# Two adds of batch 0 moved from VectorE to GpSimd, and new places for steps in a hand-written order (hourglass attention, then ELU layer, one Trainium2 core)

## Chip, cores and metric

The kernel runs on one NeuronCore of a Trainium2 chip. Its time is the device time of one launch in microseconds (us), median of several runs. Five engines work side by side, each through its own queue in order: TensorE (in the profile PE, its weight loads PEld), VectorE (DVE), ScalarE (ACT), GpSimd (POOL) and SyncE (SP, which here only issues transfers). They wait for each other by semaphores.

## What is computed

Inputs are q, k, v of 8 batches, 8 heads, 576 positions, 64 values, all float32, and two weight matrices of 512x2048 and 2048x512.

```python
q_d = q.reshape(B, H, Sd, 4, D).mean(axis=3)      # k_d, v_d likewise: 144 coarse positions
out_d = softmax_attention(q_d, k_d, v_d)          # scale 1/8
out_up = np.repeat(out_d, 4, axis=2)              # coarse part, each row four times
mask = np.abs(pos[:, None] - pos[None, :]) < 4
out_local = softmax_attention(q, k, v, mask)      # local part: a band of 7 keys
x = (out_up + out_local) as [4608, 512]           # heads side by side
h = x @ w_in
g = np.where(h > 0, h, np.exp(np.minimum(h, 0)) - 1)
out = g @ w_out
```

The sum `out_up + out_local` is the "add of the coarse to the local part" that the change speaks of.

## The kernel before

A unit of the attention is one pair of heads of one batch, `(b, j)` with b from 0 to 7 and j from 0 to 3. For each pair the kernel

- loads q and k (`load_qk`, or `load_cast`, a transfer issued by GpSimd that converts to float16 on its way) and v (`load_v`, then `cast_v` on GpSimd, line 242);
- transposes q and k on TensorE (`transposes`, lines 263 to 285) and copies the result out of PSUM on ScalarE or VectorE (lines 298, 305);
- makes scores (lines 348 to 392), exponentials on ScalarE (372, 402), and in batches 1 to 7 a multiplication with the band mask on VectorE (422);
- sums denominators on TensorE and takes reciprocals on VectorE (478 to 491 in batch 0, 437 to 452 later) and spreads them over all rows (496, 508, copies 798 and 516);
- multiplies with v (551, 558 in batch 0; 531, 539 later), normalises on VectorE (568, 584) into a float16 tile `ln`, and adds the coarse to the local columns into `xt` (574 in batch 0, 604 later).

The dense layer takes blocks of 512 tokens. `mm1(t, fc)` multiplies `xt(t)` with 128 columns of w_in (line 619 for block 0, 640 for others), then ScalarE takes an exponential `e` (644) and VectorE makes the ELU in two steps (645, 646) into `gt`. `mm2(t, i)` multiplies a quarter of `gt` with w_out (660). For block 0 the first two accumulators are filled ahead (`ahead`, line 815, four calls for the four pairs of heads).

Batch 0 runs through a front of its own in halves of 288 positions: `first_transposes`, `first_scores`, `first_v`, `first_dens`, `first_spread`, `first_outputs`, `first_normalise`. The last four have an index i; i of 0 and 1 are the pairs (0,1) and (2,3) of the first half, i of 2 and 3 the same pairs of the second half. `normalise_half` makes the adds of batch 0, and line 573 takes VectorE or GpSimd for each by a list of eight entries: entries 0 to 3 are the four i of batch 0, entries 4 to 7 are the four pairs of batch 1 (line 603, for the columns that fall into block 1).

`keep(t, n)` puts work on TensorE that nothing reads: n matmuls of 512 zero columns (line 679), or for a float16 tile 4n small transposes (line 682). The numbers n are in `FK`.

PSUM holds few tiles. The tag `two` gives two large buffers in turn once `close_front` has run, for transposed q and k, scores, spread reciprocals, `lg` (outputs) and `vs`. The tags `hp` and `misc` have two banks each.

The order of all work is written out by hand. Each step is given a time by `at(time, step)`, the steps are sorted by it, and each engine's queue follows from that order. The times themselves are nothing that the chip sees. `F` and `FK` hold those of batch 0, `PLAN` those of batches 1 to 3 (tr transposes, sc scores, cast, dn denominators, vs sums of v, sp spread, out outputs), `MM1` and `MM2` those of the dense layer, and the loads of w_out (`load_wo`) have a list of their own.

Of the kernel before, what the change touches and what calls it, by code (L numbers as in the profile page):

```python
# [15 lines left out]
B, H, S, D = 8, 8, 576, 64  # L16
# [53 lines left out]
def kernel(  # L70
# [9 lines left out]
    nc = tc.nc  # L80
# [343 lines left out]
    def by_pe(b):  # L424

        return b in [0, 1, 2]
# [137 lines left out]
    def normalise_half(js, g, lg):  # L564
        z, n = js[-1] + 1, HB + SH
        ln = sb.tile([128, RW], FP16, tag="ln", bufs=2, name="ln")
        ln = h2(ln[:])
        nc.vector.tensor_tensor(
            out=ln, in0=g2(lg[:], 0, n), in1=RB[0][:, js[0] : z, n * g : n * g + n], op=AB.mult
        )  # L570
        parts = ((0, 0, HB, 0),) if g == 0 else ((0, 0, TBLK - HB, HB), (1, TBLK - HB, HB, 0))
        for t, a, b_, to in parts:
            eng = nc.vector if t == 0 and [1, 1, 1, 0, 0, 0, 0, 1][2 * g + js[0] // 2] else nc.gpsimd
            eng.tensor_tensor(
                out=xt(t)[:, js[0] : z, to : to + b_ - a].rearrange("p j (u f) -> p j u f", f=4),
                in0=ln[:, :, a:b_].rearrange("p j (u f) -> p j u f", f=4),
                in1=_rep4(ln[:, :, HB + a // 4 : HB + b_ // 4]), op=AB.add,
            )

    def normalise(b, j, lg):  # L580
        rcb = RB[b]
        ln = sb.tile([128, RW], FP16, tag="ln", bufs=2, name="ln")
        if by_pe(b):
            nc.vector.tensor_tensor(  # L584
                out=h2(ln[:]), in0=g2(lg[:], 0, HB + SH), in1=h2(rcb[:, j, :]), op=AB.mult
            )
        else:
            nc.vector.tensor_tensor(
                out=ln[:, S:RW], in0=lg[:, HB : HB + SD], in1=rcb[:, j, S:RW], op=AB.mult
            )  # L590
            nc.vector.tensor_tensor(  # L591
                out=h2(ln[:, 0:S]), in0=g2(lg[:], 0, HB), in1=h2(rcb[:, j, 0:S]), op=AB.mult
            )
        t0 = S * b
        while t0 < S * (b + 1):
            t = t0 // TBLK
            t1 = min(TBLK * (t + 1), S * (b + 1))
            a, z = t0 - S * b, t1 - S * b
            if by_pe(b) and a < HB < z:
                z, t1 = HB, S * b + HB  # L600
            h = a // HB if by_pe(b) else 0
            la, ga = (a + SH * h, HB + HB * h + a // 4) if by_pe(b) else (a, S + a // 4)
            eng = nc.vector if (b, t) == (1, 1) and [1, 1, 1, 0, 0, 0, 0, 1][4 + j] else nc.gpsimd
            eng.tensor_tensor(  # L604
                out=xt(t)[:, j, t0 - TBLK * t : t1 - TBLK * t], in0=ln[:, la : la + z - a],
                in1=_rep4(ln[:, ga : ga + (z - a) // 4]), op=AB.add,
            )
            t0 = t1
        st.pop((b, j))
# [63 lines left out]
    Z = sb.tile([128, 512], FP16, tag="Z", bufs=1, name="Z")  # L673
# [165 lines left out]

    at(-100, first)  # L840
    at(-65, second)
    F = dict(T=[-41.13, -39.95, -36.66, -32.16], S=[-39.2, -35.63, -33.39, -30.84], Z=[-32.52, -32.14, -32.14, -28.4], V=[-33.32, -30.92, -30.71, -27.94], P=[-29.75, -28.02, -20.88, -18.53], O=[-30, -26.95, -20.73, -13.92], N=[-28.12, -24.72, -19.09, -13.8], H=[-24.18, -20.45, -18.09, -17.91], lv=[-52.45, -36.44, -34.49, -32.17], cv=[-36.2, -33.27, -32.43, -29.76], lw=[-30, -29.11, -20.29, -11.97], rp=[-28.54, -23.88, -22.41, -14.05], D=[-32.62, -29.37, -29.34, -24.56], wi=[-33.19, -32.56, -30.01, -29.05], cf=[-29.29], k=[-41.47, -35.38, -33.37, -28.21])
    FK = dict(Tq=[1, 0, 0, 0], Tk=[0, 0, 2, 0], S=[1, 0, 2, 1], Z=[1, 0, 2, 0], P=[0, 1, 0, 0], O=[1, 4, 0, 2], D=[0, 0, 0, 0])
    for j in range(NPAIR):
        at(F["T"][j], first_transposes, j, (FK["Tq"][j], FK["Tk"][j]))
        at(F["S"][j], first_scores, j, 0, FK["S"][j])
# [24 lines left out]
        spread_copy(b, j, rb, copy)  # L871

    MM1 = [[-14.19, 1.09, 0.706], [19.14, 0.992], [35.73, 1.018], [51.52, 1.02]]
    MM2 = [[14.98, 0.794], [34.5, 1.095], [51.68, 1.02]]

    def mm1_at(t, i):
        if t == 0:
# [10 lines left out]
    def load(n):  # L888
# [2 lines left out]
            load_v(*pairs[n])  # L891

    PLAN = {
        1: dict(tr=[-12.21, -5.594, -1.76, -1.482], sc=[-7.07, 0.103, 0.888, 2.276], cast=[-23.96, -13.31, -12.32, 1.701], dn=[16.38], vs=[15.62], sp=[18.61, 18.14, 18.46, 18.98], out=[18.98, 18.52, 18.54, 18.99], so=[10.57], si=[10.03]),
        2: dict(tr=[8.521, 19.14, 20.81, 24.84], sc=[16.66, 21.68, 23.15, 26.21], cast=[6.002, 15.82, 19.12, 20.36], dn=[28.71], vs=[29.1], sp=[30.02, 30.15, 29.43, 32.38], out=[30.72, 32.86, 33, 33.03], so=[17.79], si=[28.4]),
        3: dict(tr=[25.32, 29.24, 30.74, 34.58], sc=[28.69, 32, 36.48, 37.89], cast=[21.15, 25.5, 25.89, 28.85], dn=[40.9], vs=[40.84], so=[41.77], si=[43.95], out=[46.72, 47.24, 48.76, 48.78]),
    }
    LATER = dict(tr=[-27.78, -24.81, -17.34, -16.19], sc=[-25.74, -22.03, -14.56, -12.79], cast=[-32.93, -27.69, -22.54, -19.07], dn=[-10.25], vs=[-10.47], so=[-9.791], si=[-6.96], out=[-4.288, -4.511, -3.148, -3.906])
    LAST = dict(tr=[-27.36, -24.54, -17.71, -14.25], sc=[-25.67, -22.06, -15.67, -11.26], cast=[-32.18, -27.83, -24.84, -20.85], dn=[-9.492], vs=[-9.098], so=[-9.367], si=[-5.664], out=[-2.829, -4.665, -4.912, -2.635])
# [3 lines left out]
    for b in range(1, B):  # L903
        p = PLAN[b]
        for j in range(NPAIR):
            n = NPAIR * (b - 2) + j
# [18 lines left out]
                at(p["out"][js[0]], pair_outputs, b, js)  # L925
    for n, x in enumerate([-8.454, -6.202, 3.581]):
        at(x, load, n)
    for n, x in enumerate([-21.48, -3.996, 1.576, 2.844]):
        at(x, load_wo, n)
    for t in range(NT):  # L930
        for i in range(16):
# [35 lines left out]
```

## Time and profile before

| | |
|---|---|
| median of 3 runs | 357.72 us (356.89 to 359.48) |
| the profiled execution | 356.68 us, span from first to last instruction 354.8 us |
| mean granted TensorE clock | 0.995 |
| DVE, ACT, POOL busy | 247.1, 200.0, 167.6 us |
| TensorE idle in the first 140 us / after it | 12.9 / 3.3 us |

The last row is the length of the stretches less PE's busy time in them. The profile is of one execution. It tells per instruction when it began, how long it took, how long its engine sat idle before it and what ended the wait. The chain of waits follows the work back from the last instruction; "issue" in it is time for which no releaser is seen. Some loads of this part, from the queue of transfers that GpSimd issues: w_in is loaded in four parts (WI, issued between 15.42 and 19.95 us), w_out in four (WO, issued at 35.86, 47.38, 51.78 and 53.50).

### The profile page before, as it was taken

Reading aid. Unit: us, or ns where it says so; the run is one execution under the profiler, and the core shown is the slowest. Engines: PE = TensorE matmul, PEld = TensorE weight load, DVE = VectorE, ACT = ScalarE, POOL = GpSimd, SP = SyncE. Lnnn points to the kernel's source line nnn. Section 1 sums busy time; section 2 is a strip of 40 time slices with the busy share of each in tenths; the row PEclk is TensorE's granted clock in tenths of the full one; section 3 lists DMA queues with packets and bytes.
Section 4 is the critical chain, followed back from the end, with each engine's and each line's share of the span. In section 5 each row is a group of like instructions: output and inputs, shape, how many; then the busy total and the mean of one; then the engine's idle time right before and its main releaser. Section 6 shows DMA issues by size and latency. Waiting matters only on the chain.

```text
span 354.8 us, 8863 instructions
## 1 busy us (share of the span) xinstructions
PE 338.6 (95%) x3520; PEld 191.6 (54%) x3520; DVE 247.1 (70%) x452; ACT 200.0 (56%) x368; POOL 167.6 (47%) x305
## 2 busy tenths in 40 slices
PE   8887998899979999999999999999999999999996
PEld 4665886555555555555555555555555544444443
DVE  2316998676898868887997799879766855555510
ACT  3572798457775754677476736773664444444421
POOL 4534658596877744954595459846200500000000
PEclk9998999999999999999999999999999999999999
DMA  8999999999794958686968698461004010010012
GB/s 180 179 191 200 189 201 217 226 216 229 170 203 92 228 147 164 144 219 152 188 166 217 151 179 202 110 142 35 31 32 117 32 59 30 31 59 30 31 59 89
DMA packets 100322, 49.12 MB, mean 138 GB/s; under 512 B 81770, under 2 KB 95290, under 8 KB 100282
## 3 DMA queue, kind: packets, MB, share of 16 engines
q1 hardware_dynamic: 94442, 42.20, 53.1%
q0 software_dynamic: 5600, 6.26, 10.6%
q8 instruction: 27, 0.44, 0.6%
q10 hardware_dynamic: 240, 0.11, 0.2%
q14 instruction: 13, 0.11, 0.1%
HBM read 42.24 MB, written 9.62 MB: 146 GB/s over the span
## 4 chain that ended last, share of the span: by engine, by line
PE 88%; DVE 5%; ACT 4%; issue 2%; DVEq 0%; ACTq 0%
PE op L660 35%; PE hp L640 31%; PE sc L382 3%; PE lg L531 2%; PE hp L619 2%; PE sc L679 2%; PE tqk L268 2%; ACT pex L402 1%; PE sc L392 1%; PE vs L338 1%; DVE ln L584 1%; DVE gt L646 1%; PE lg L539 1%; PE den L437 1%; ACT e L644 1%
## 5 line engine op out<-in xcount | busy, mean ns | idle before, releaser
L660 PE MATMUL op<-WO,gt 128*128 128x512 f16 (+2 forms) x592 | 145.3, 374 | 0.0
L644 ACT ACTIVATE e<-hp 128x512 f16<-128x512 f32 x144 | 86.3, 602 | 91.8 <-PE hp L640 78.2
L640 PE MATMUL hp<-xt,WI 128*128 128x512 f16 x512 | 132.0, 380 | 0.7 <-DVE xt L604 0.6
L646 DVE SCALAR_TENSOR_TENSOR gt<-hp,e 128x512 f16<-128x512 f32 x144 | 99.6, 692 | 6.4
L660 PEld LDWEIGHTS <-gt 128*128 128x128 f16 x592 | 55.2, 98 | 61.6 <-issue 0.9
L645 DVE TENSOR_SCALAR e<-e 128x512 f16<-128x512 f16 x144 | 60.1, 417 | 40.2 <-ACT e L644 39.5
L640 PEld LDWEIGHTS <-WI 128*128 128x128 f16 x512 | 55.0, 114 | 48.2
L604 POOL TENSOR_TENSOR xt<-ln 128x128 f16<-128x128 f16 (+10 forms) x62 | 37.4, 632 | 48.7 <-DVE ln L591 41.1
L402 ACT ACTIVATE pex<-sc 112x576 f16<-112x576 f32 x112 | 50.0, 528 | 10.6 <-PE sc L392 10.5
L329 POOL TENSOR_TENSOR t<-qt 128x288 f32<-128x288 f16 x27 | 18.2, 672 | 39.4 <-ACT qt L298 39.4
L422 DVE TENSOR_TENSOR pex<-pex,MASK 112x1152 f16<-112x1152 f16 x28 | 23.8, 851 | 15.5 <-ACT pex L402 15.3
L242 POOL CAST v<-v 112x768 f16<-112x768 f32 x32 | 27.0, 844 | 12.2 <-DMA v<-in_v_dram 12.2
L666 ACT COPY os<-op 128x512 f32<-128x512 f32 (+2 forms) x37 | 21.4, 578 | 18.3 <-PE op L660 18.1
L323 DVE TENSOR_REDUCE kd<-kt 128x144 f16<-128x576 f16 x28 | 20.8, 744 | 1.1 <-ACT kt L305 1.1
L298 ACT COPY qt<-tqk 128x576 f16<-128x576 f16 x28 | 18.0, 644 | 5.9 <-PE tqk L268 5.1
L205 POOL CAST k<-k 96x768 f16<-96x768 f32 x24 | 20.4, 848 | 0.1
L205 POOL CAST q<-q 96x768 f16<-96x768 f32 x24 | 19.7, 821 | 0.2 <-issue 0.2
L382 PEld LDWEIGHTS <-kt 64*112 64x112 f16 x336 | 11.3, 127 | 12.4 <-issue 11.6
L619 PE MATMUL hp<-xt,WI 128*128 128x256 f16 x128 | 17.0, 283 | 0.5 <-DVE v L217 0.4
L382 PE MATMUL sc<-qt,kt 64*112 64x96 f16 x336 | 14.7, 217 | 1.5 <-ACT pex L402 1.3
L331 POOL TENSOR_TENSOR qd<-t 128x144 f16<-128x144 f32 x27 | 14.0, 519 | 2.1
L591 DVE TENSOR_TENSOR ln<-lg,rcb 128x576 f16<-128x576 f32 x20 | 15.0, 748 | 0.0
(111 smaller groups left out, 291.5 us busy)
## 6 DMA issues: line engine op xcount, KB each, us to landing
v<-in_v_dram SPq DMA_DIRECT2D x30, 336.0 KB, 6.0
out_dram<-os SPq DMA_DIRECT2D x35, 256.0 KB, 2.1
q<-in_q_dram SPq DMA_DIRECT2D x25, 288.0 KB, 3.5
k<-in_k_dram SPq DMA_DIRECT2D x25, 288.0 KB, 4.3
rcb<-rd SPq DMA_DIRECT2D x10, 360.0 KB, 5.2
WI<-in_moe_w_in_dram POOLq DMA_DIRECT2D x4, 512.0 KB, 9.6
WO<-in_moe_w_out_dram POOLq DMA_DIRECT2D x4, 512.0 KB, 7.8
q<-in_q_dram POOLq DMA_DIRECT2D x7, 144.0 KB, 7.1
```

The lines of the kernel that those rows point to most:

```text
L205: nc.gpsimd.tensor_copy(out=x[:], in_=src)
L242: nc.gpsimd.tensor_copy(out=v16[:], in_=v32[:].rearrange("p (e c) d -> p c e d", e=2))
L382: nc.tensor.matmul(sc[e][0:KW, a : a + QB], s["kt"][r, KO - PAD + QB * c :][:, 0:KW], s["qt"][c][r], start=True, stop=True,)
L402: nc.scalar.activation(out=s["p"][0:rows, e, :, a : a + n], in_=g2(sc[0:rows], a, n), func=AF.Exp, scale=SCALE / 16 if b and a == HB else ...
L422: nc.vector.tensor_tensor(out=to, in0=to, in1=mk2, op=AB.mult)
L604: eng.tensor_tensor(out=xt(t)[:, j, t0 - TBLK * t : t1 - TBLK * t], in0=ln[:, la : la + z - a], in1=_rep4(ln[:, ga : ga + (z - a) // 4]), ...
L619: nc.tensor.matmul(FS[i][:, 256 * f : 256 * f + 256], w_in(dc, 2 * n + f), xts[0][:, dc, 256 * h : 256 * h + 256], start=(f == dc == 0), s ...
L640: nc.tensor.matmul(hp, w_in(dc, fc), xts[t][:, dc, :], start=(dc == 0), stop=(dc == DMC - 1),)
L644: nc.scalar.activation(out=e, in_=hp, func=AF.Exp)
L645: nc.vector.tensor_scalar(out=e, in0=e, scalar1=1.0, scalar2=-1.0, op0=AB.min, op1=AB.add)
L646: nc.vector.scalar_tensor_tensor(out=to, in0=hp, scalar=0.0, op0=AB.max, in1=e, op1=AB.add)
L660: nc.tensor.matmul(op_[:, a:z], gts[t][:, fc, 128 * tt : 128 * tt + 128], WO[:, fc, a:z], start=(fc == 0), stop=(fc == FCN - 1),)
```

## The change

Two entries of the list on lines 573 and 603 go from 1 to 0, the tables of times get new values, and three numbers of `FK` change.

```diff
--- before.py
+++ after.py
@@ -570,7 +570,7 @@
         )
         parts = ((0, 0, HB, 0),) if g == 0 else ((0, 0, TBLK - HB, HB), (1, TBLK - HB, HB, 0))
         for t, a, b_, to in parts:
-            eng = nc.vector if t == 0 and [1, 1, 1, 0, 0, 0, 0, 1][2 * g + js[0] // 2] else nc.gpsimd
+            eng = nc.vector if t == 0 and [0, 1, 0, 0, 0, 0, 0, 1][2 * g + js[0] // 2] else nc.gpsimd
             eng.tensor_tensor(
                 out=xt(t)[:, js[0] : z, to : to + b_ - a].rearrange("p j (u f) -> p j u f", f=4),
                 in0=ln[:, :, a:b_].rearrange("p j (u f) -> p j u f", f=4),
@@ -600,7 +600,7 @@
                 z, t1 = HB, S * b + HB
             h = a // HB if by_pe(b) else 0
             la, ga = (a + SH * h, HB + HB * h + a // 4) if by_pe(b) else (a, S + a // 4)
-            eng = nc.vector if (b, t) == (1, 1) and [1, 1, 1, 0, 0, 0, 0, 1][4 + j] else nc.gpsimd
+            eng = nc.vector if (b, t) == (1, 1) and [0, 1, 0, 0, 0, 0, 0, 1][4 + j] else nc.gpsimd
             eng.tensor_tensor(
                 out=xt(t)[:, j, t0 - TBLK * t : t1 - TBLK * t], in0=ln[:, la : la + z - a],
                 in1=_rep4(ln[:, ga : ga + (z - a) // 4]), op=AB.add,
@@ -839,8 +839,8 @@
 
     at(-100, first)
     at(-65, second)
-    F = dict(T=[-41.13, -39.95, -36.66, -32.16], S=[-39.2, -35.63, -33.39, -30.84], Z=[-32.52, -32.14, -32.14, -28.4], V=[-33.32, -30.92, -30.71, -27.94], P=[-29.75, -28.02, -20.88, -18.53], O=[-30, -26.95, -20.73, -13.92], N=[-28.12, -24.72, -19.09, -13.8], H=[-24.18, -20.45, -18.09, -17.91], lv=[-52.45, -36.44, -34.49, -32.17], cv=[-36.2, -33.27, -32.43, -29.76], lw=[-30, -29.11, -20.29, -11.97], rp=[-28.54, -23.88, -22.41, -14.05], D=[-32.62, -29.37, -29.34, -24.56], wi=[-33.19, -32.56, -30.01, -29.05], cf=[-29.29], k=[-41.47, -35.38, -33.37, -28.21])
-    FK = dict(Tq=[1, 0, 0, 0], Tk=[0, 0, 2, 0], S=[1, 0, 2, 1], Z=[1, 0, 2, 0], P=[0, 1, 0, 0], O=[1, 4, 0, 2], D=[0, 0, 0, 0])
+    F = dict(T=[-40.88, -39.39, -36.09, -31.59], S=[-38.63, -35.07, -32.82, -29.94], Z=[-31.95, -31.57, -31.56, -27.84], V=[-32.75, -30.35, -30.14, -27.19], P=[-29.2, -27.45, -20.31, -17.62], O=[-29.43, -26.38, -20.16, -13.36], N=[-27.33, -24.16, -19.23, -13.23], H=[-23.61, -19.88, -17.52, -17.2], lv=[-52.73, -36.61, -34.54, -32.22], cv=[-35.63, -32.7, -31.61, -29.19], lw=[-29.43, -28.54, -19.72, -11.4], rp=[-27.17, -23.16, -21.13, -13.34], D=[-32.05, -28.8, -28.77, -24], wi=[-32.62, -31.99, -29.44, -28.48], cf=[-28.72], k=[-35.99, -34.56, -32.8, -27.19])
+    FK = dict(Tq=[1, 0, 0, 0], Tk=[0, 0, 3, 0], S=[1, 0, 2, 1], Z=[1, 0, 2, 0], P=[0, 1, 0, 0], O=[1, 3, 0, 0], D=[0, 0, 0, 0])
     for j in range(NPAIR):
         at(F["T"][j], first_transposes, j, (FK["Tq"][j], FK["Tk"][j]))
         at(F["S"][j], first_scores, j, 0, FK["S"][j])
@@ -871,7 +871,7 @@
         spread_copy(b, j, rb, copy)
 
     MM1 = [[-14.19, 1.09, 0.706], [19.14, 0.992], [35.73, 1.018], [51.52, 1.02]]
-    MM2 = [[14.98, 0.794], [34.5, 1.095], [51.68, 1.02]]
+    MM2 = [[14.98, 0.794], [34.5, 1.091], [51.68, 1.02]]
 
     def mm1_at(t, i):
         if t == 0:
@@ -891,9 +891,9 @@
             load_v(*pairs[n])
 
     PLAN = {
-        1: dict(tr=[-12.21, -5.594, -1.76, -1.482], sc=[-7.07, 0.103, 0.888, 2.276], cast=[-23.96, -13.31, -12.32, 1.701], dn=[16.38], vs=[15.62], sp=[18.61, 18.14, 18.46, 18.98], out=[18.98, 18.52, 18.54, 18.99], so=[10.57], si=[10.03]),
-        2: dict(tr=[8.521, 19.14, 20.81, 24.84], sc=[16.66, 21.68, 23.15, 26.21], cast=[6.002, 15.82, 19.12, 20.36], dn=[28.71], vs=[29.1], sp=[30.02, 30.15, 29.43, 32.38], out=[30.72, 32.86, 33, 33.03], so=[17.79], si=[28.4]),
-        3: dict(tr=[25.32, 29.24, 30.74, 34.58], sc=[28.69, 32, 36.48, 37.89], cast=[21.15, 25.5, 25.89, 28.85], dn=[40.9], vs=[40.84], so=[41.77], si=[43.95], out=[46.72, 47.24, 48.76, 48.78]),
+        1: dict(tr=[-12.26, -5.594, -4.144, -1.294], sc=[-7.07, 0.103, 0.888, 5.814], cast=[-24.58, -13.94, -12.95, 1.024], dn=[16.38], vs=[16.2], sp=[18.91, 18.14, 18.46, 18.98], out=[18.98, 18.52, 18.54, 18.99], so=[11.7], si=[10.03]),
+        2: dict(tr=[8.521, 19.14, 20.81, 24.93], sc=[16.66, 21.68, 23.3, 26.36], cast=[6.002, 15.72, 19.12, 20.36], dn=[28.71], vs=[29.1], sp=[30.02, 30.15, 29.43, 32.38], out=[30.72, 32.86, 32.86, 33.03], so=[18.95], si=[33.02]),
+        3: dict(tr=[25.32, 29.24, 30.74, 34.58], sc=[28.69, 32, 36.48, 37.89], cast=[21.15, 25.5, 25.89, 28.85], dn=[40.9], vs=[40.84], so=[41.03], si=[43.42], out=[46.54, 47.06, 48.57, 48.6]),
     }
     LATER = dict(tr=[-27.78, -24.81, -17.34, -16.19], sc=[-25.74, -22.03, -14.56, -12.79], cast=[-32.93, -27.69, -22.54, -19.07], dn=[-10.25], vs=[-10.47], so=[-9.791], si=[-6.96], out=[-4.288, -4.511, -3.148, -3.906])
     LAST = dict(tr=[-27.36, -24.54, -17.71, -14.25], sc=[-25.67, -22.06, -15.67, -11.26], cast=[-32.18, -27.83, -24.84, -20.85], dn=[-9.492], vs=[-9.098], so=[-9.367], si=[-5.664], out=[-2.829, -4.665, -4.912, -2.635])
@@ -925,7 +925,7 @@
                 at(p["out"][js[0]], pair_outputs, b, js)
     for n, x in enumerate([-8.454, -6.202, 3.581]):
         at(x, load, n)
-    for n, x in enumerate([-21.48, -3.996, 1.576, 2.844]):
+    for n, x in enumerate([-21.48, -4.346, 1.576, 2.844]):
         at(x, load_wo, n)
     for t in range(NT):
         for i in range(16):
```

What becomes of the order, step by step:

- Adds: entries 0 and 2 go to GpSimd, so the adds of i=0 (128x576 elements) and i=2 (128x448) of batch 0. The entries of batch 1 keep their values.
- Filling work: `first_transposes(2)` gets 12 small transposes for 8; `first_outputs(1)` three matmuls of 512 columns for four; `first_outputs(3)` none for two.
- Front, SP's queue: the constant VR (7 KB) is loaded behind v of pair 1 and not ahead of it.
- Front, PE's and ACT's queues: `first_v(2)` goes ahead of `first_scores(3, 0)`. VectorE: the small reduction for the constant FOUR (line 752) goes behind the first `ln`.
- Front, GpSimd's queue: the add of i=0, then the constant FOUR, now stand ahead of `load_cast(1, 0)`. `load_wo(0)` goes ahead of `load_cast(1, 2)`; the adds of i=2 and `cast_v(1, 1)` go ahead of `load_cast(1, 3)`.
- Batch 1: `pair_transposes(1, 2)` goes ahead of `mm1(0, 9)` and `mm1(0, 10)`. `pair_scores(1, 3)` goes behind `mm1(0, 15)`. `v_batch(1)` goes behind `mm2(0, 1)`. `cast_v(1, 3)` goes ahead of `load_wo(2)`.
- Batch 3: `pair_outputs(3, (2, 3))` goes ahead of `mm2(1, 13)`.
- The other new times (those of `first_transposes` among them) leave the order of each engine's instructions as it was.

## Prediction

> **What bounds the kernel now.** I read the page's busy times and slices first, then the chain of waits, then windows of the front, then each engine's queue in order of time.
>
> ```profile
> PE 338.6 (95%) x3520; PEld 191.6 (54%) x3520; DVE 247.1 (70%) x452; ACT 200.0 (56%) x368; POOL 167.6 (47%) x305
> PEclk9998999999999999999999999999999999999999
> q8 instruction: 27, 0.44, 0.6%
> PE 88%; DVE 5%; ACT 4%; issue 2%; DVEq 0%; ACTq 0%
> ```
>
> TensorE sets the time: 95% busy, 88% of the chain. Its idle time is 12.9 us before 140 us and 3.3 us after, so a change of order can win or lose only in the first 140 us. Every edit that moves an engine's instructions but one lies before 63 us; the exception is mm2(1, 13) at 138.5. One slice has a lower clock. The third line is PE's own instructions: 27 packets, 0.44 MB, so 16 KB each, for 3520 loads and 3520 matmuls, some 260 a packet.
>
> The chain in the front (start, length, what):
>
> ```profile
> 23.34 0.14 PE rb L496
> 23.48 1.14 issue
> 24.61 0.45 PE rb L496 x9
> ...
> 29.10 0.03 PE den L485 x2
> 29.13 1.96 issue
> 31.09 0.30 PE den L485 x6
> ```
>
> Two stops of 1.14 and 1.96 us in the middle of a row of matmuls, with no releaser. They are waits for instructions. In the trace's list of weight loads, 221, 349 and 477 loads stand ahead of the places where PE resumes at 17.47, 24.62 and 31.09: 128 matmuls with their loads, one packet, apart. The packets of the instruction queue land at 16.10, 23.04 and 29.54, each 1.4 to 1.6 us ahead of the resuming. The windows around the second stop (us, PE, PEld, DVE, ACT, POOL busy, clock, DMA):
>
> ```profile
> 27.71:31.12 3.41, 1.45 (x46) 0.81 (x45) 2.20 (x3) 0.48 (x2) 0.00 (x0) 1.00 1.23 196
> 31.12:34.53 3.41, 3.41 (x44) 2.68 (x44) 1.20 (x3) 0.76 (x1) 2.16 (x4) 0.50 1.25 222
> 34.53:37.94 3.41, 3.27 (x70) 2.77 (x68) 3.21 (x6) 1.60 (x3) 3.33 (x7) 1.00 1.19 162
> ```
>
> After a stretch with PE busy for 1.45 of 3.41 us, the clock is halved for 3.41 us: 1.7 us lost. Behind that VectorE binds until 41.5, PE again until 48.3, then ScalarE's exponentials alternate with PE until 57.7.
>
> ```profile
> 36.38 0.29 DVE L645 TENSOR_SCALAR e<-e 128x512 f16<-128x512 f16 x1
> 39.13 0.74 DVE L323 TENSOR_REDUCE qd<-qt 128x144 f16<-128x576 f16 x1
> ...
> 54.83 1.25 ACT pex L402 x3
> 56.12 0.46 PE sc L382 x11
> 56.71 1.00 PE hp L619 x8
> 57.74 0.67 PE tqk L268 x12
> ```
>
> **The change part by part**, against the profiled execution (356.68: span 354.8 plus 1.9 around it).
>
> *Fills in the front.* Eight small transposes (L682) take 0.55 on the chain, so four more cost 0.27. They stand between packet borders 93 and 221: PE reaches border 221 no sooner than its packet, and all the loss until then is eaten by the wait at 24.62, whose end depends on the packet alone (it starts 4.7 after the crossing at 17.47, in the company of the w_in loads, which are the same in both kernels). The same border then comes four matmuls earlier in the work, so four L558 of 0.02 each follow the wait. At the second stop it comes three earlier (one fill is gone): three L485 at half clock, 0.05 each, are left over. Sum +0.1. If packets came at once the cost were 0.27; if the border fell badly, 0.3. The dropped fill of i=1 (0.26) ends in the same stop: nothing. The two of i=3 (0.59) are followed by a wait of matmul hp at 37.53 for gt L646 (until 37.47), and qt L298 before it feeds only qd L323, which VectorE reaches at 39.13: nothing.
>
> *Two adds.* VectorE loses 0.76 (L574, 128x576, at 27.49) and 0.63 (128x448, at 34.88). The first lies ahead of an idle 0.72 us. The second lies ahead of rcb L798 (35.42), which would end 0.35 earlier; but e at 36.38 follows ScalarE's e (35.75 to 36.36), which follows PE. So no gain, unless PE's part shrinks, then up to 0.6. On GpSimd, rows of L574 are 0.95 for 448 columns and 0.39 to 0.42 for 128, so 576 take 1.2 as an estimate: from 27.4 to 28.6 with GpSimd idle, read by PE's hp at 31.39, 2.8 spare. The second runs from some 36.0 (behind three transfers' issue) with its 128-column partner until 37.5, and `cast_v(1, 1)` and the adds of i=3 follow; mm1(0, 8) reads them at 44.92, the adds end by 41.5.
>
> What it costs is VectorE's time beside it. Step e (L645) is 0.28 to 0.30 in all 65 cases with no GpSimd instruction beside it, and with an add of L604 beside it 0.29 to 0.86, mean 0.59 over 15. Beside the add of L574 in this front the two rows are 0.28 and 0.29, by luck of the moment.
>
> ```profile
> 137.56 2.64 POOL L604 TENSOR_TENSOR xt<-ln 128x320 f16<-128x320 f16 x4 [4.47 <-DVE ln L591]
> 138.28 0.76 DVE L645 TENSOR_SCALAR e<-e 128x512 f16<-128x512 f16 x1
> ```
>
> In the changed order GpSimd works without rest from 36 to 42, where three e stand at 36.38, 38.21 and 40.45, all on VectorE's binding stretch. Bounds: none meets, 0; all three at the worst row, 1.7. I take two at the mean excess of 0.30: +0.6. The Trainium skill, "GPSIMD Engine Reference", section 8, says that GpSimd shares its SBUF interfaces with VectorE and contends with VectorE's two-port modes and two SBUF inputs; it speaks against the change. The trace agrees for e (by the rule the term lies in the upper half, by the two rows of L574 at 0); gt (L646) is 0.69 in all its rows beside GpSimd or not, so gt costs nothing here.
>
> *Loads moved.* VR goes behind v(0,1) on SP's queue and takes over its wait for an earlier transfer; IND and the next v stand behind that wait. VR is read at 16.14, and IND, queued behind it, landed at 14.9: nothing. `load_cast(1, 0)` was issued at 19.95 and 20.59, but its packets (768 bytes) began only at 29.9, behind WI; now it waits for the add and FOUR, and is issued at 29.4 to 30.7. Behind the waiting add on GpSimd's queue are FOUR, this load and `cast_v(1, 0)`, which waited until 31.97 for its data anyway. The load is read by tqk L263 at 36.71 (36.2 now). Casts issued between 30 and 40 took 4.6 to land: 35.3, hidden. The casts of pairs 2 and 3 go behind WO's part 0 (128 packets, some 3 us) and two adds; the first landed near 38.6, lands near 42 and is read at 45.8, the last is read at 49.2, issued at 39: hidden. FOUR is read at 64. WO of part 2 goes 1.0 later, behind a cast (0.84) and its 0.18; it landed at 59.4 and is read at 61.6; part 3 landed at 62.0 and is read at 63.14. Some 0.6 later it still lands in time: nothing, else up to 1.
>
> *Batch 1.* `pair_transposes(1, 2)` comes 1.8 earlier; ScalarE then reaches e of (0, 11) when PE ends it (49.28, before 49.40), so kt L305 and sc at 51.19 come 0.1 earlier: −0.1. (In the front, `first_v(2)` puts a copy of 0.36 ahead of an exponential whose first reader stands behind the stop at 24.62: nothing.) `pair_scores(1, 3)` and `mm1(0, 15)` change places. Before, PE waits 0.64 and more for the exponentials of pair 2 (until 56.07), then hp (56.71) covers the wait for pair 3's. Now hp goes into the first gap, sc still starts at 56.1, but ScalarE makes e of (0, 15), 0.61, ahead of pair 3's exponentials, and tqk needs their buffer: 57.1 plus 0.9, so 58.0 for 57.74. +0.3. The swap of vs and mm2(0, 1) and the one at 138.5 (lg's buffer was free at 138.36) cost nothing.
>
> Sum: +0.1 +0.6 −0.1 +0.3 = +0.9, so 357.6 for this execution. It lies 1.04 below the median, so 358.6.
>
> The Trainium skill, "TensorE: Matmul & The Clock Gate", section "What's actually happening", says that the window of activity is 3.413 us and runs freely. The half-clock row agrees in length (3.41); the sentence before that an idle window is needed does not, since PE worked 1.45 us in it. By a free phase the 1.7 us come and go between executions of one kernel.
>
> **The rivals.**
>
> *Slower: the first load of batch 1 comes late.* Place: tqk L263, k's part at 36.9 us, with mm1(0, 2) and all of PE behind it. For it: the casts' median over the whole span is 7.2 from issue, and the old load took 12.5 from 20.59 to 33. Against: what delayed the old one was WI, gone by 30.2. It decides if it lands after 36.9, and makes the kernel slower by over 1% past 39.6, 8.9 behind its issue at 30.7. Price: at 7.2 (37.8), 0.9; at 12.5 (43.1), 6.2: 359.5 to 364.8. Chance of over 1%: 0.11.
>
> *Faster: the second stop vanishes.* Its packet waits 4.0 us from crossing to start, in the company of w_in. If GpSimd's later load frees the engines before 28.66, the stop (1.96) and the half clock (1.7) go: 3.7 off the median, 354.0, and the other terms add −0.4 to +0.9: 353.6 to 354.9. Against: the old load's packets began at 29.9, after the instruction packet. 0.08, half of it beyond one per cent.
>
> *No change: VectorE's relief is worth its contention.* If the meetings of e miss (0) and the 0.35 of rcb count, +0.3 −0.35: 357.7. It is nearest to the two rows of L574. 0.11.
>
> *The change does less than it says.* For batch 1 it does: its four entries keep their values, so no add of batch 1 moves. That is in the sum.
>
> **How the numbers follow.** Forecast 0.70, no change 0.11, late load 0.11, vanished stop 0.08. Predicted 358.6. Low end: sum at −0.4 (no meetings, rcb counted, no loss at sc) on the lowest run shown, 356.89: 356.5. High end: port 1.7, WO 1.0, sc 0.3 and front 0.3 give +3.3 on the median: 361.0. The 0.19 of the two outer rivals lie outside. Within one per cent (3.6 us, about what a measurement of this kernel can tell from no change) lie forecast, no change and half the vanished stop, 0.70 + 0.11 + 0.04: faster 0.04, same 0.85, slower 0.11.
>
> **What would show it.** Right: stops at the same two borders, resuming near 24.6 and 31.1; e between 36 and 41 longer than 0.30 at least twice; tqk of (2, 0) some 0.3 behind its old place relative to sc of (1, 3) ending. Wrong: PE waiting at tqk near 36 for a transfer; a stop of another length, or another half-clock stretch; e at 0.29 throughout and VectorE still earlier at 41.5.

## The result, and the profile after

The changed kernel takes 360.37 us (median of 20 runs, 358.20 to 361.60), the kernel before, run beside it, 358.35 (20 runs). The ratio is 1.0066, 95% interval [1.0046, 1.0086]: slower by two thirds of a per cent, about 2.4 us. (Ratios here leave out runs more than 1.5% above the fastest of their kernel; where that takes out half of a changed kernel's runs, the median over all stands beside it.) The profiled execution took 360.88 us, its span 359.0.

First the page of the changed kernel: busy times, granted clock by slices, the instruction queue, the chain's shares.

```profile
PE 338.8 (94%) x3521; PEld 192.3 (54%) x3521; DVE 246.5 (69%) x450; ACT 199.8 (56%) x368; POOL 170.2 (47%) x307
...
PEclk9998799999989999999999999999999999999999
...
q8 instruction: 27, 0.44, 0.5%
...
PE 80%; DMA 6%; DVE 6%; ACT 2%; issue 2%; POOL 1%; SPq 0%; DVEq 0%; POOLq 0%; ACTq 0%
```

PE is busy for as long as before (338.8 against 338.6), and the span is 4.2 longer. Its idle time in the first 140 us is 16.9 us for 12.9: nearly the whole difference of the two executions is idle PE there. In the chain, transfers have come in (6%) and PE's share has gone from 88% to 80%. Of the 4.2 us, only 2.0 are the difference of the medians: the profile of before is of an execution 1.67 us faster than its median of 358.35, that of the changed kernel of one 0.51 slower than its own.

Next the chain through the front (start, length, what), and PE's rows in order of time around the same place:

```profile
18.80 11.89 DMA WI<-in_moe_w_in_dram
30.70 3.80 issue
34.50 1.01 PE hp L619 x4
```
```profile
27.59 0.21 PE L478 MATMUL den<-pex,IND 112*32 112x72 f16 x1 [0.93 <-issue]
27.60 0.27 PE L485 MATMUL den<-pex,IND 96*32 96x72 f16 x8
27.80 0.63 PE L619 MATMUL hp<-xt,WI 128*128 128x256 f16 x4
...
34.50 1.01 PE L619 MATMUL hp<-xt,WI 128*128 128x256 f16 x4 [5.23 <-issue]
```

The same second group of L619 before, then the last issue of w_in and the times from issue to landing of its four parts, first before, then after:

```profile
33.75 0.97 PE L619 MATMUL hp<-xt,WI 128*128 128x256 f16 x4
...
19.21 0.74 POOL L137 DMA_DIRECT2D WI<-in_moe_w_in_dram  x1
DMA to landing us min/median/max: 5.5/9.6/12.4
...
20.30 0.75 POOL L137 DMA_DIRECT2D WI<-in_moe_w_in_dram  x1
DMA to landing us min/median/max: 7.7/11.2/14.1
```

"Border n" is the place in PE's work with n weight loads ahead of it; PE crosses it when it starts the next one. The two stops before were at borders 349 and 477. As in the forecast, the start of the packet for border 349 is counted from PE's crossing of border 221, one packet earlier.

The two stops for instructions are gone but for 0.93 us at border 477: the packets land at 13.93, 18.36 and 26.07 (16.10, 23.04 and 29.54 before), the first two ahead of PE. The first `ahead` starts at 27.80, 3.5 us earlier than before. The second starts at 34.50, later than before (33.75): PE stands still for 5.23 us. The view names no releaser, but the semaphores kept in the trace do: here PE's queue waits for those of the second, third and fourth part of w_in, and the last one landed at 34.4, issued at 20.30. This group reads columns of the first part alone, as the first `ahead` does, and the first `ahead` waited for the first part alone. The same wait stands in the kernel before; there PE came to it, delayed by its stops, when w_in had landed (31.6; the forecast had it gone by 30.2). So the stops and the wait for w_in lay over each other, and w_in was late, too: the cast of v(0, 0), which stands ahead of w_in on GpSimd's queue, began at 13.67 and not at 11.55, since its data landed later.

The windows around it (us, busy PE, PEld, DVE, ACT, POOL, granted clock, DMA), and one later pair:

```profile
29.48:32.89 3.41, 0.00 (x0) 0.00 (x0) 0.91 (x1) 0.07 (x1) 3.08 (x6) 1.00 1.24 206
32.89:36.30 3.41, 1.80 (x16) 1.48 (x17) 0.15 (x1) 0.00 (x0) 1.35 (x3) 0.50 1.35 211
36.30:39.71 3.41, 3.41 (x53) 2.58 (x51) 2.30 (x4) 1.11 (x3) 1.94 (x4) 0.50 1.11 201
39.71:43.12 3.41, 3.41 (x32) 3.36 (x32) 3.27 (x7) 2.85 (x5) 1.69 (x3) 1.00 0.99 149
101.10:104.50 3.40, 2.40 (x22) 1.59 (x22) 3.37 (x6) 1.76 (x4) 3.13 (x8) 1.00 1.22 236
104.55:107.96 3.41, 3.41 (x38) 1.95 (x39) 2.48 (x4) 1.28 (x3) 1.58 (x5) 0.51 1.53 212
```

One wait of 5 us in one piece leaves PE idle for a whole window and for half of the next, and the clock is halved for two windows (6.8 us, the first 1.6 of them still within the wait) instead of one. At 104.6 a third half-clock window follows a stretch with PE busy for 2.40 of 3.40 us. It is not the change's own: eight of the fourteen profiles of this study have 3.4 or 6.8 us of half clock near 100 us, among them z2, z3 and y4 below, which are variants of the kernel before; the profile of before has none.

Last, VectorE's e of block 0 and GpSimd's instructions beside it, in order of time:

```profile
47.80 1.40 POOL L329 TENSOR_TENSOR t<-qt 128x288 f32<-128x288 f16 x1 [3.10 <-ACT qt L298]
...
48.39 0.29 DVE L645 TENSOR_SCALAR e<-e 128x512 f16<-128x512 f16 x1
...
49.28 0.42 POOL L331 TENSOR_TENSOR qd<-t 128x144 f16<-128x144 f32 x1
...
50.07 1.02 DVE L645 TENSOR_SCALAR e<-e 128x512 f16<-128x512 f16 x1
...
50.25 0.68 POOL L329 TENSOR_TENSOR t<-qt 128x288 f32<-128x288 f16 x1
```

The e of 0.28 to 0.30 takes 1.02 us beside t (L329), and an earlier t takes 1.40 for the usual 0.66. The long e ends at 51.09, 0.16 after that t (50.93). Two more e are 0.45 (44.15) and 0.47 (54.45). The three e between 38 and 43, where the forecast had seen contention, are 0.28 to 0.30. Over the sixteen e of block 0 the excess over 0.285 is 1.10 us (0.31 before).

How far the changed kernel lies behind the kernel before at the same matmul: +0.74 us at the second `ahead`, +2.04 at mm1(0, 2), +1.70 at mm1(0, 6), +2.78 at the scores of (2, 0), constant until 99 us, +4.2 behind the half-clock window at 104.6.

### The profile page after: what moved, and what is told of

The parts are those of the page before. It is cut to its first block, busy times and chain, and to the rows that moved or that the text cites. A ratio compares the mean times of both kernels' runs of the same rounds, so it can differ in the third digit from the quotient of the medians.

```text
span 359.0 us, 8865 instructions
## 1 busy us (share of the span) xinstructions
PE 338.8 (94%) x3521; PEld 192.3 (54%) x3521; DVE 246.5 (69%) x450; ACT 199.8 (56%) x368; POOL 170.2 (47%) x307
## 4 chain that ended last, share of the span: by engine, by line
PE 80%; DMA 6%; DVE 6%; ACT 2%; issue 2%; POOL 1%; SPq 0%; DVEq 0%; POOLq 0%; ACTq 0%
PE op L660 35%; PE hp L640 31%; DMA WI<-in_moe_w_in_dram 3%; DMA v<-in_v_dram 3%; PE sc L382 3%; PE lg L531 2%; DVE gt L646 2%; PE hp L619 2%; PE tqk L268 2%; DVE e L645 1%; ACT pex L402 1%; PE sc L392 1%; PE lg L539 1%; PE den L437 1%; PE vs L338 1%
## 5 line engine op out<-in xcount | busy, mean ns | idle before, releaser
L640 PEld LDWEIGHTS <-WI 128*128 128x128 f16 x512 | 55.4, 115 | 48.6 <-issue 0.6
L329 POOL TENSOR_TENSOR t<-qt 128x288 f32<-128x288 f16 x27 | 19.3, 714 | 38.3 <-ACT qt L298 38.3
L619 PE MATMUL hp<-xt,WI 128*128 128x256 f16 x128 | 17.3, 288 | 5.6 <-issue 5.2
L382 PEld LDWEIGHTS <-kt 64*112 64x112 f16 x336 | 11.2, 129 | 12.9 <-issue 11.2
L619 PEld LDWEIGHTS <-WI 128*128 128x128 f16 x128 | 13.7, 117 | 6.9 <-issue 5.6
```

Of the source, the lines that this page charges most:

```text
L382: nc.tensor.matmul(sc[e][0:KW, a : a + QB], s["kt"][r, KO - PAD + QB * c :][:, 0:KW], s["qt"][c][r], start=True, stop=True,)
L619: nc.tensor.matmul(FS[i][:, 256 * f : 256 * f + 256], w_in(dc, 2 * n + f), xts[0][:, dc, 256 * h : 256 * h + 256], start=(f == dc == 0), s ...
L640: nc.tensor.matmul(hp, w_in(dc, fc), xts[t][:, dc, :], start=(dc == 0), stop=(dc == DMC - 1),)
```

## The experiments

Each ran five rounds beside the kernel before, 12 runs each. In "wait", "lag" and "excess" I give for each profile: PE's idle time before the second `ahead`; how much its lag behind the profile of before grew between mm1(0, 6) and the scores of (2, 0); the excess of block 0's sixteen e. A profile is of one execution, and some are of one well off their kernel's median: x1's took 357.62 us, z2's 360.83.

**Parts taken back, one at a time, out of the changed kernel.**

x1, VR ahead of v(0, 1) again:

```diff
-k=[-35.99, -34.56, -32.8, -27.19]
+k=[-41.47, -34.56, -32.8, -27.19]
```


> The changed kernel with the load of VR put back ahead of v of pair 1 on SP's queue, nothing else. Theory W (late w_in): with v(0,1) issued at 3.3 us at once behind v(0,0), v(0,0) lands 2 us later, so GpSimd's cast of it, and behind it on GpSimd's queue the four w_in loads, start 1.1 us later, and the second call of ahead, which waits for all four, stops PE from 29.3 to 34.5. Put back: cast of v(0,0) near 11.6 instead of 13.7, last w_in issue near 19.2 instead of 20.3, last w_in landing near 31.6, PE's wait ahead of the second group of L619 under 1 us; ratio to before 1.002 to 1.004 (batch 1's order still costs about 1 us). Rival O (batch 1's order and contention are the cost, the late landing is chance): cast anywhere between 11 and 14 as before, ratio 1.006 to 1.007.

Measured 360.89 us, 1.0064 [1.0027, 1.0101]. The cast of v(0, 0) began at 11.41 and w_in landed by 32.3 (31.6 before); PE still waited 3.36 us at the second `ahead`, and the clock was halved for 6.8 us. The ratio is rival O's, though the interval reaches down to theory W's: VR's place isn't shown to cost anything, and with w_in 2.1 us earlier most of the wait was still there.

x2, both adds on VectorE again:

```diff
-[0, 1, 0, 0, 0, 0, 0, 1]
+[1, 1, 1, 0, 0, 0, 0, 1]
```


> The changed kernel with both adds of batch 0 back on VectorE. Theory W: the adds lie behind the w_in issues on GpSimd's queue and beside idle time, so PE's wait ahead of the second L619 group stays at several us and the ratio stays within 0.002 of the changed kernel's 1.0066. Rival P (the adds on GpSimd are the cost, by the delay of the loads queued behind them or by contention with VectorE's e): ratio falls to 1.003 or less.

Measured 359.50 us, 1.0039 [1.0011, 1.0068]; wait 4.63, lag +0.45 (+1.08 with the adds on GpSimd). The wait stays, as theory W had it; the ratio lies between the two forecasts, and the interval overlaps the change's own. The excess is as large as the changed kernel's (1.12), with an e of 1.02 us at mm1(0, 8) here, too: that e doesn't come from the adds.

y1, the fill back at eight transposes:

```diff
-Tk=[0, 0, 3, 0]
+Tk=[0, 0, 2, 0]
```


> The changed kernel with the fill of first_transposes(2) back at 8 small transposes for 12. In the profile of before, PE crossed border 221 at 17.47 and the packet for border 349 started at 22.16, behind w_in's packets that had begun at 16.9; in the changed kernel it crossed at 16.56 and the packet started at 17.09, ahead of w_in's, which began at 18. Theory (who is first in the queue decides, and not the number of fills): the border moves by 0.27 us of work, the crossing stays ahead of 18, the packet starts before 18, and no stop of over 0.3 us comes back at border 349; PE still waits 4 to 5 us for w_in at the second ahead; ratio 1.005 to 1.008, as the change's own 1.0066. Rival (the four extra transposes took the stops away): a stop of 1 us or more is back at border 349, the wait at the second ahead is under 2.5 us, ratio 1.006 or less since the stop and the wait lie in the same time.

Measured 360.70 us, 1.0058 [1.0034, 1.0082]. The packet for border 349 started at 17.64, within 0.5 of the crossing, and no stop came back there; at border 477 PE stopped for 1.26 (0.93 in the changed kernel); wait 4.88. The rival falls: the four transposes are not what took the stop at border 349 away in the profile of the changed kernel.

y2, batch 1 in its old order:

```diff
-tr=[-12.26, -5.594, -4.144, -1.294], sc=[-7.07, 0.103, 0.888, 5.814], vs=[16.2]
+tr=[-12.26, -5.594, -1.76, -1.294], sc=[-7.07, 0.103, 0.888, 2.276], vs=[15.62]
```


> The changed kernel with pair_transposes(1, 2), pair_scores(1, 3) and v_batch(1) at the places that they had before. Theory: the new places cost 1.1 us between mm1(0, 6) and the scores of (2, 0) (the lag behind before grew there from 1.70 to 2.78 in the profiles); without them it doesn't grow by more than 0.3, and the ratio falls from 1.0066 to 1.003 to 1.004. Rival 1 (my prediction's price, +0.2 for the two swaps, the rest being contention of GpSimd with e that another order also meets): the lag still grows by 0.8 or more, ratio 1.0055 to 1.0066. Rival 2: the price was chance of one execution, ratio unchanged and lag constant.

Measured 360.30 us, 1.0053 [1.0028, 1.0078]; the lag still grew by 0.99, and the excess was 2.16, on other e than in the changed kernel. Rival 1's trace, and a ratio just below its range: the order of batch 1 alone does not carry this stretch.

```profile
43.24 0.92 DVE L645 TENSOR_SCALAR e<-e 128x512 f16<-128x512 f16 x1
...
50.77 0.51 DVE L645 TENSOR_SCALAR e<-e 128x512 f16<-128x512 f16 x1
...
53.65 0.89 DVE L645 TENSOR_SCALAR e<-e 128x512 f16<-128x512 f16 x1
...
55.91 0.89 DVE L645 TENSOR_SCALAR e<-e 128x512 f16<-128x512 f16 x1
```

**Single parts put into the kernel before.**

y4, the fill alone:

```diff
-Tk=[0, 0, 2, 0]
+Tk=[0, 0, 3, 0]
```


> The kernel before with 12 small transposes for 8 in first_transposes(2), nothing else. Theory (first in the queue decides): w_in's packets begin at 17, border 221 is crossed at 17.1 to 17.5 or little earlier, so the packet for border 349 still starts behind them, after 20, and the stops of 1 to 2 us at borders 349 and 477 stay; ratio 0.9985 to 1.0015. If the crossing falls ahead of 16.8, the packet starts at once and the stop goes even here. Rival (the fill takes the stops away): the packets start within 1 us of the crossing, no stop over 0.3 us; PE then waits 2 to 3.5 us for w_in at the second ahead, and the ratio is 0.995 to 1.000, as the wait ends at 32.5 to 33.5 at the earliest against 33.75.

Measured 359.10 us, 1.0013 [0.9986, 1.0039]. Its profile has the front of the changed kernel (PE in order of time):

```profile
27.41 0.21 PE L478 MATMUL den<-pex,IND 112*32 112x72 f16 x2 [0.47 <-issue]
27.41 0.27 PE L485 MATMUL den<-pex,IND 96*32 96x72 f16 x8
27.61 0.63 PE L619 MATMUL hp<-xt,WI 128*128 128x256 f16 x4
...
34.62 1.02 PE L619 MATMUL hp<-xt,WI 128*128 128x256 f16 x4 [5.54 <-issue]
```

The stop at 349 is gone, that at 477 nearly, and the wait for w_in is there, but not by the fill alone: without it, y1 has no stop at 349 either. The cast of v(0, 0) began at 13.94 here, with loads in the order of before. Border 221 was crossed at 16.50, and w_in's packets began at 18.93; the packet for border 349 started at 17.31. Over all fourteen profiles of this study one pattern holds for this packet: where PE crosses border 221 by 0.6 us or more ahead of w_in's first packets (after: 16.56 against 18.58; x1: 16.39 against 17.06), the packet for border 349 starts 0.2 to 0.8 us after the crossing; where it crosses closer to them or behind them (before: 17.47 against 16.89; z5: 16.02 against 16.47; also x4, y3 and z3 below), it starts after 2.6 to 4.7 us. Other packets differ: that for border 221 starts 0.7 to 3.1 us after the crossing of border 93, which lies over 5 us ahead of w_in's packets, and that for border 477, with w_in in flight, 2.3 to 4.0 us after the crossing of 349 in all profiles.

z1 and z2, the adds alone and batch 1's order alone:

```diff
-[1, 1, 1, 0, 0, 0, 0, 1]
+[0, 1, 0, 0, 0, 0, 0, 1]
```


> The kernel before with the two adds of batch 0 on GpSimd and everything else as it was. Theory (the change is slower by a sum of small prices, the adds' among them): taking the adds back out of the changed kernel moved the ratio from 1.0066 to 1.0039, so putting them into the kernel before costs about the same, 1.001 to 1.004, and steps e between 36 and 52 us take 0.5 us or more longer in sum than in the profile of before (0.31 over the 16 steps of block 0). Rival (VectorE's relief is worth its contention): 0.998 to 1.001. What the two say together: if the price is in the adds, this run and the one with the adds back agree; if it is in the moved loads and the order, this run is at 1.000.

```diff
-tr=[-12.21, -5.594, -1.76, -1.482], sc=[-7.07, 0.103, 0.888, 2.276], vs=[15.62]
+tr=[-12.21, -5.594, -4.144, -1.482], sc=[-7.07, 0.103, 0.888, 5.814], vs=[16.2]
```


> The kernel before with only the three new places of batch 1: pair_transposes(1, 2) ahead of mm1(0, 9), pair_scores(1, 3) behind mm1(0, 15), v_batch(1) behind mm2(0, 1). Theory: the new order puts GpSimd's t of pair 2 (L329) beside e of mm1(0, 8), as in all profiles with this order and the adds in either place (e 1.01 to 1.02 for 0.28); e of (0, 8) takes about 1.0 here too and the scores of (2, 0) come 0.5 to 1.1 later: ratio 1.0015 to 1.003. Rival (the new order only exchanges one meeting for another, as the changed kernel with the old order still had 2.16 us of excess in its sixteen e): ratio 0.999 to 1.001.

z1: 358.63 us, 1.0004 [0.9962, 1.0046]; lag 0.00, excess 0.29. z2: 357.58 us, 0.9978 [0.9942, 1.0015]; lag +0.17, excess 0.59. Neither is shown to cost anything by itself: z1's theory of a price in the adds alone falls by its trace (its ratio doesn't exclude it), z2's by ratio and trace; its e of mm1(0, 8) did grow, to 0.68. Both profiles have the wait for w_in (5.24 and 4.98 us), 10.2 and 6.8 us of halved clock around it, and a stop of 1.11 and 1.02 at border 477.

z5, the rest of the change without these four parts (VR, adds, fill, batch 1):

```diff
-k=[-35.99, -34.56, -32.8, -27.19]
+k=[-41.47, -34.56, -32.8, -27.19]
-[0, 1, 0, 0, 0, 0, 0, 1]
+[1, 1, 1, 0, 0, 0, 0, 1]
-Tk=[0, 0, 3, 0]
+Tk=[0, 0, 2, 0]
-tr=[-12.26, -5.594, -4.144, -1.294], sc=[-7.07, 0.103, 0.888, 5.814], vs=[16.2]
+tr=[-12.26, -5.594, -1.76, -1.294], sc=[-7.07, 0.103, 0.888, 2.276], vs=[15.62]
```


> The changed kernel with four parts taken back: the adds on VectorE, the three places of batch 1, the fill of first_transposes(2) at 8, VR ahead of v(0, 1). What is left of the change: the loads and casts moved on GpSimd's queue (load_cast(1, 0) behind FOUR, WO's part 0 ahead of load_cast(1, 2), cast_v(1, 1) ahead of load_cast(1, 3), cast_v(1, 3) ahead of WO's part 2), FOUR's reduction, first_v(2), the three fills dropped from first_outputs, and pair_outputs(3, (2, 3)). Theory A (the price of about 2 us sits in this rest, since each of the four parts, taken back or put in alone, moved the ratio by 0.0027 at most and by -0.0022 to +0.0013 put in): ratio 1.003 to 1.006, and the mean granted clock of its runs is below the 0.989 of the kernel before, near the 0.985 of the changed one. Theory B (the price is a sum of small ones, none in the moved loads, as the prediction had them at nothing): ratio 0.999 to 1.002, clock as before. Theory C (the parts only cost together, each taking cover from the other): also 0.999 to 1.002, which this run can't tell from B.

Measured 357.94 us (356.43 to 358.45), 0.9983 [0.9967, 0.9999]. Theory A falls, by the clock too (a mean of 0.9871 over the runs here and beside it): this rest of the change costs nothing and, if anything, saves about 0.6 us. The ratio lies a little below what theories B and C gave. Here a stop for instructions and the wait for w_in shared the time (PE in order of time):

```profile
26.13 0.21 PE L485 MATMUL den<-pex,IND 96*32 96x72 f16 x3
28.22 0.24 PE L485 MATMUL den<-pex,IND 96*32 96x72 f16 x5 [1.88 <-issue]
28.39 1.04 PE L619 MATMUL hp<-xt,WI 128*128 128x256 f16 x4
...
32.03 1.02 PE L619 MATMUL hp<-xt,WI 128*128 128x256 f16 x4 [1.13 <-issue]
```

Its lag didn't grow in batch 1 (0.00), and its excess is 0.29. It is the one kernel of the study whose interval lies below 1, by 0.0001.

**The waits taken away.** x3 and x4 hold w_in in four tiles of 512 columns, so that a matmul waits for its own part alone (code lines move up by one):

```diff
-    WI = sb.tile([128, DMC, DFF], FP16, tag="WI", bufs=1, name="WI")
+    WI = [sb.tile([128, DMC, 512], FP16, tag=f"WI{i}", bufs=1, name="WI") for i in range(4)]
-        a = 512 * (fc // 4) + fc % 4
-        return WI[:, dc, a : a + 509 : 4]
+        return WI[fc // 4][:, dc, fc % 4 : fc % 4 + 509 : 4]
-        nc.gpsimd.dma_start(out=WI[:, :, a:z], in_=src)
+        nc.gpsimd.dma_start(out=WI[a // 512][:], in_=src)
```


> The changed kernel with w_in held in four tiles of 512 columns, so that each use waits for its own part's load alone. Theory W: the second group of L619 no longer waits for the last part; PE's stop of 5.2 us shrinks to under 1 us, the half clock after it goes or shrinks, and the time falls by 2 to 4 us: ratio 0.996 to 1.001. Rival O: PE then waits as long a little later (for VectorE's chain or the q and k of batch 1), ratio stays at 1.005 to 1.007.

> The kernel before with w_in in four tiles in the same way. In the profile of before the last part landed at 31.6 and the second L619 group ran at 33.75, so that wait was covered by the stops for instructions. Theory W with the wait covered: ratio 0.998 to 1.000. If the wait binds before too in executions without the stops: ratio 0.993 to 0.997.

x3 (the changed kernel): 358.54 us, 1.0021 [0.9993, 1.0049]. x4 (the kernel before): 357.73 us, 0.9979 [0.9946, 1.0012]. In both the wait at the second `ahead` is gone (28.86 in x3, for 34.50). But in x3 the next wait stands behind it (PE in order of time):

```profile
33.87 0.45 PE L262 MATMUL tqk<-ID,q 96*64 96x96 f16 x12 [2.66 <-DMA q<-in_q_dram]
34.98 0.45 PE L262 MATMUL tqk<-ID,k 96*64 96x96 f16 x12 [0.66 <-DMA k<-in_k_dram]
```

This is the late `load_cast(1, 0)`, and behind it came an e of 1.99 us (at 37.83) beside GpSimd's adds of i=3 (38.26 to 39.59), which stand on GpSimd in the kernel before, too. From 4.9 us ahead of the kernel before at the second `ahead`, x3 falls back to 2.2 at mm1(0, 2), 0.9 at mm1(0, 6) and nothing at the scores of (2, 0).

y3, x3 with that load back ahead of the add and FOUR:

```diff
-rp=[-27.17, -23.16, -21.13, -13.34]
+rp=[-28.4, -23.16, -21.13, -13.34]
```


> The changed kernel with w_in in four tiles (so that a quarter's matmuls wait for one part only) and load_cast(1, 0) ahead of the add of i=0 and FOUR on GpSimd, as before. With the four tiles alone the ratio was 1.0021 [0.9993, 1.0049], and PE then waited 2.77 us at tqk L263 for q of (1, 0), landed 33.8, and 0.66 for k. Theory (my rival of the late load, which the wait for w_in had hidden): PE waits under 0.7 us for these two, mm1(0, 2) starts 1.5 to 3 us earlier than 35.35, ratio 0.995 to 0.999. Rival (VectorE beside GpSimd's adds binds there: e took 1.99 us at 37.83 beside an add): the wait goes, but e, the adds or their readers are late by as much at mm1(0, 8), ratio 1.001 to 1.003.

Measured 359.61 us, 1.0016 [0.9983, 1.0050]. PE no longer waits for q or k, but in this profile the clock was halved from 10.7 to 20.9 us, border 221 was crossed late (20.93), and the lag grew by 1.38 in batch 1, with e of 0.86 and 1.38: the rival's e and the rival's ratio, though the interval reaches into the theory's range.

z3, the kernel before in four tiles, parts 1 to 3 issued behind `load_cast(1, 0)` and FOUR:

```diff
-wi=[-33.19, -32.56, -30.01, -29.05]
+wi=[-33.19, -28.5, -27.9, -26.9]
```


> The kernel before with w_in in four tiles, and with parts 1 to 3, which are first read at mm1(0, 4), mm1(0, 8) and mm1(0, 12), issued behind load_cast(1, 0) and FOUR instead of from 16 us on. Theory (the instruction packets wait behind w_in's packets, and the front is held by w_in, the packets and load_cast(1, 0) in turn): with a quarter of w_in in flight the packets for borders 349 and 477 land ahead of PE, no stop over 0.7 us is left, q of (1, 0) lands before 28, the second ahead starts before 31 (33.75 before) and mm1(0, 2) before 35 (37.53): 2.5 to 5 us, ratio 0.986 to 0.994. Rival 1 (VectorE's normalising binds as soon as the waits are gone): the second ahead is early, mm1(0, 8) less than 1 us early, ratio 0.996 to 1.000. Rival 2 (parts 1 to 3 come late): PE waits for w_in at mm1(0, 4) near 37, ratio above 1.

Measured 0.9957 [0.9910, 1.0004] over 6 of its 12 runs; the median of all 12 is 359.41 against 358.95, so no gain is shown. Its trace does what the theory said: packets land at 22.15 and 26.73, the second `ahead` starts at 29.90, mm1(0, 2) at 33.77, 3.76 us ahead of the kernel before, and this holds until 53 us. Then it is given back (PE in order of time):

```profile
57.05 1.02 PE L659 MATMUL op<-WO,gt 128*128 128x512 f16 x4 [0.30 <-DMA WO<-in_moe_w_out_dram]
...
59.74 1.02 PE L659 MATMUL op<-WO,gt 128*128 128x512 f16 x4 [0.79 <-DMA WO<-in_moe_w_out_dram]
...
62.71 1.02 PE L659 MATMUL op<-WO,gt 128*128 128x512 f16 x4 [1.38 <-DMA WO<-in_moe_w_out_dram]
```

Of the lead, 3.2 us are gone by mm1(1, 0), 2.5 of them in these waits for w_out, whose last part is there no sooner than before (62.7 against 62.0), and 2.0 are lost between 96 and 111 us, where the clock is halved; the lead of 3.76 is then a lag of 1.46. That w_out sooner would keep the lead was not tried.

## Why the prediction was right or wrong

A sum of +0.9 us was forecast, in a range from 356.5 to 361.0; the ratio makes it +2.4, inside the range, within one per cent, and the right way. The terms did not come out as they were priced, so that the time came out near is in part luck.

**The front: the step that failed.** "all the loss until then is eaten by the wait at 24.62, whose end depends on the packet alone", with w_in's loads "the same in both kernels". This took the two stops of one execution for a property of the order. They depend on when PE crosses border 221 and when w_in's packets begin, and the kernel before with four transposes (y4), with the adds (z1) and with batch 1's order (z2) had the other outcome in its profile: no stop at border 349, and 5.0 to 5.5 us of wait for w_in. Most of the 2.04 us at mm1(0, 2) therefore seems to belong to the two executions: y4, z1 and z2 lie 2.0 to 3.2 us behind the profile of before at that place, with medians that are not shown to be slower. The forecast's own signs of being wrong came here: a stop of another length and a further half-clock stretch. What makes the cast of v(0, 0) start at 11.1 to 11.8 us in some and at 13.6 to 14.2 in others stays open; both are seen with VR in either place.

**The faster rival** said that without the second stop 3.7 us are gained. It did shrink to 0.93, and nothing was gained, for what that rival left out: the next wait on PE's queue, for all of w_in, ended at 33.75 before and at 34.50 after. The row at 33.75 stood in the profile of before with no idle time ahead of it, and the semaphores of its weight load would have shown it. x3 and x4 show that the single tile makes this wait. Taking it out moves the changed kernel by −0.45% (1.0066 to 1.0021), just clear of the two intervals, and the kernel before by −0.21%, which is not.

**Contention of GpSimd with e** (+0.6): right in kind, wrong in place. The e at 38 to 43 were not touched; those of batch 1, at 44 to 56, were, beside t and casts that stand behind the adds on GpSimd's queue. Nor is a slow e a slowed one, as the mean excess took it: over the fourteen profiles 604 of the 605 e that took over 0.4 us end 0.15 to 0.23 us after a GpSimd instruction does. So the price of a meeting goes by what is left of that instruction. All six profiles with the adds on GpSimd inside the changed order (after, x1, x3, y1, y2, y3) lose 0.93 to 1.38 us there against before; with the adds back on VectorE (x2) 0.45, with the adds alone in the old order (z1) 0. So in these profiles some 1 us is lost where the adds meet the moved order. The excess of e alone doesn't account for it, since x2 has as much excess and half the lag; and x2 and z1 are one execution each, so the adds' share isn't shown. The Trainium skill, "GPSIMD Engine Reference", section 8, says that GpSimd shares its SBUF interfaces with VectorE and contends with VectorE instructions in a two-port mode or with two SBUF inputs; the rows of e agree (0.28 alone, up to 1.99), and GpSimd's t is stretched, too (1.40 for 0.66). The steps gt stayed at 0.69, as the forecast had it.

**Batch 1's order** (+0.2): not confirmed. Alone it is −0.22% [−0.58, +0.15], taken back −0.13%, within the intervals.

**Loads moved** (nothing): right in sum, z5 is 0.9983. The load was mis-sized: its two halves took 8.2 and 8.6 us to land for the 4.6 that was taken, from issues at 26.99 and 27.65. The late `load_cast(1, 0)`, my slower rival, is real (2.66 and 0.66 us in x3), and it cost nothing in the profile of the changed kernel only because the wait for w_in covered it.

**Fills** (+0.1): 1.0013 alone, 0.08% taken back; both agree with 0.1 us, and their intervals with nothing.

**The clock.** The forecast said that 1.7 us of half clock "come and go between executions". They do, but not evenly. Over all runs that list a clock, the kernel before has a mean of 0.9876 (116 runs, mean 358.53 us), the changed kernel 0.9848 (20 runs, 360.18), the four kernels with one part taken back 0.9837 (48 runs). The share lost, (1 − clock) times the time, is 4.4 us before and 5.5 after: about 1.0 of the 1.65 us between the means, if all of it lies on the path. Among the 116 runs of the kernel before, a run with a mean clock lower by 0.01 took 2.1 us longer and not the 3.6 of this sum; at that rate the share is an estimated 0.6. In x3, without the wait for w_in, the mean is 0.9882. That the lower clock comes from this wait is not shown: z1 and z2, whose profiles have the same wait, have means of 0.9881 and 0.9907.

**What stays open.** With the rest of the change at 0.9983, the four parts cost 0.8% together. Taken back one at a time they sum to 0.5%, three of them put in alone to nothing (−0.05%); each figure is uncertain by 0.2 to 0.4%. They seem to cost only in company. That they do so through GpSimd's queue in batch 1 and the wait for w_in is argued and not shown, and with these uncertainties a plain sum of four small prices isn't excluded. VR alone in the old order wasn't tried. So the cause of the 0.66% stays open.

## What to carry to other kernels

A stall that is seen in one profile may cover the next one: before a price is put on its end, list every wait of the instructions behind it and when each would have ended. Here the stops covered w_in, w_in covered the late load, and with all three gone w_out took the lead back. Check whether a stall is of the order or of the execution: a second profile, or a kernel that differs in a place that can't matter, tells it. And a reader of a tile that is loaded in parts can wait for parts that it doesn't read, as the second `ahead` did; separate tiles took that wait away here.

## What was not expected of the hardware

An idle stretch of PE cost more than its length: 5.23 us came with 6.8 us at half clock, 5.2 of them behind it. The length doesn't follow from one piece or two: the two stops of 1.14 and 1.96 were followed by 3.41 us at half clock, those of 1.88 and 1.13 in z5 by 6.8, those of 0.88 and 1.68 in x4 by none. The windows follow each other without a gap, and a window with PE busy for 2.40 of 3.40 us was followed by half clock, as was one with 1.45 in the kernel before, so no window without work is needed. Nor does the busy time alone decide: the window from 53.37 to 56.78 in the changed kernel, with PE busy for 2.10 us, was followed by full clock.

A VectorE step e that took over 0.4 us ended 0.15 to 0.23 us after a GpSimd instruction, however long it was (604 of 605 in the fourteen profiles); the longest before 60 us, 1.99 us in x3, sat beside two adds in a row.

The 16 KB packet of instructions for border 349 started 0.2 to 0.8 us after the crossing of border 221 when w_in's packets were still 0.6 us off, and 2.6 to 4.7 us after it otherwise; other packets do not follow this pattern.
